# Six token groups of 384 in place of nine of 256 in the last MoE block of a fused attention and MoE kernel

## The chip, the cores and the metric

The kernel runs on one core of one Trainium2 chip. The metric is the device time of one execution in microseconds (us), given as a median over runs; smaller is better.

## What is computed

Banded and pooled attention over `q`, `k`, `v` gives a matrix `x` of 2304 tokens by 512. A first MoE block (512 to 1024 to 512, with a soft-LU and a layer norm between its two products) is applied to it, and then the block that the change touches:

```
def _moe2_ref(x, w_in, w_out):      # x: 2304 x 512, w_in: 512 x 2048, w_out: 2048 x 512
    h = x @ w_in
    g = h * np.cos(h)
    return (g @ w_out).astype(np.float32)
```

## The kernel before

All products of the two MoE blocks are made in three matmuls (`mm3`): each operand is split into a high and a low fp32r part (`split`: ScalarE copies the high part, VectorE subtracts it from the source), and high by high, high by low and low by high are added up in PSUM.

The last block goes through the tokens in groups of `GT = 256`, nine of them, and in each group through the 16 tiles (`KF2`) of 128 hidden columns. One such pair (group, tile) is called a step here; there are 144. `h2(g, m)` makes one tile of `h` with `KD = 4` times `mm3`, 12 matmuls whose moving operand is 256 tokens wide. Then seven instructions in a chain turn it into `g`: ScalarE L825 (scaled copy to integer), VectorE L826, ScalarE L828 (Sin) and L829 (Square), VectorE L830, and the split, ScalarE L368 and VectorE L369. The split result lands in a ring of `RING = 4` slots in `Gh` and `Gl`. `o2(g, m)` multiplies it with the second weight: for each 128 tokens one `mm3` with a moving operand 512 wide, so 6 matmuls, which accumulate over the 16 tiles in the PSUM tiles `oa` and `ob`. After the last tile ScalarE copies the results (L845) to `X`, and the SP queue sends them out. The program issues `h2` two steps ahead of `o2` (`LAG = 2`).

The split input of a group lies in `xh`/`xl`; a second buffer lies in the unused half of `Gh`/`Gl` (`xs`), so the split of the next group is issued in the middle of the current one.

While the first group of this block runs, `w2o_step` still loads and converts the second weight into `R1`, which held the weights of the first block, and before that the first weight goes into `w2i_h`/`w2i_l`. The last work of the first MoE block on PE is `x2`, which reads `Gh`/`Gl`.

The order on each engine is not the program's. `arrange` builds the graph of dependences, prices each instruction with a formula, works out due times, tries list schedules forwards and backwards for `ROUNDS = 20` rounds, and fixes the best order on every engine. A change of shapes therefore moves instructions elsewhere too. Lines 376 to 378 are the three matmuls of `mm3`, which all products share, so the trace is read by tile names (`h2a`, `h2b`, `oa`, `ob`, and `x` for `x2`).

Of the kernel before, what the change touches and what calls it, by code (L numbers as in the profile page):

```python
# [8 lines left out]
F32 = mybir.dt.float32  # L9
F32R = mybir.dt.float32r  # L10
# [10 lines left out]
QB = 64  # L21
# [9 lines left out]
LAG, RING = 2, 4  # L33
# [279 lines left out]
def kernel(  # L313
# [16 lines left out]
    NT, DM = out.shape  # L330
    DFF = w1i.shape[1]
    DFF2 = w2i.shape[1]
    KD = DM // 128
    KF = DFF // 128
    KF2 = DFF2 // 128
    NG = NT // GT
# [6 lines left out]
    wts = Turns(ctx.enter_context(tc.tile_pool(name="wts", bufs=1)), 1)  # L343
    moe = Turns(ctx.enter_context(tc.tile_pool(name="moe", bufs=2)), 2)
# [13 lines left out]
    w2o_s = R1.rearrange("p (k a f) -> p k a f", k=KF2, a=2)  # L358

    X = wts.tile([128, NT // QB, KD, QB], F32, name="X")  # L360
    Gh = wts.tile([128, KF, GT], F32R, name="Gh")
    Gl = wts.tile([128, KF, GT], F32R, name="Gl")
    xs = [[moe.tile([128, 2, KD, 128], F32R, name=f"x{j}", bufs=1) for j in "hl"]]

    def split(hi, lo, src, gain=None):

        if gain is None:
            nc.scalar.activation(out=hi, in_=src, func=AF.Copy)  # L368
            nc.vector.tensor_tensor(out=lo, in0=src, in1=hi.bitcast(F32), op=ALU.subtract)  # L369
        else:  # L370
            nc.scalar.activation(out=hi, in_=src, func=AF.Copy, scale=gain)
            nc.vector.scalar_tensor_tensor(out=lo, in0=src, scalar=gain, in1=hi.bitcast(F32),
                                           op0=ALU.mult, op1=ALU.subtract)

    def mm3(ps, lh, ll, rh, rl, start, stop):
        nc.tensor.matmul(ps, lh, rh, start=start, stop=False)  # L376
        nc.tensor.matmul(ps, lh, rl, start=False, stop=False)  # L377
        nc.tensor.matmul(ps, ll, rh, start=False, stop=stop)  # L378
# [8 lines left out]
    def bank(name):  # L387
        tag, bufs = BANKS[name]
        if tag in late:

            late[tag] += 1
            if late[tag] % 4 >= 2:
                tag = {"h1": "s", "m": "t"}[tag]
        return psum.tile([128, 512], F32, tag=tag, name=name, bufs=bufs)
# [204 lines left out]
    H = {}  # L599
    TB = 128 // QB  # L600

    def xsplit(g, t, d):

        x0 = (2 * g + t) * TB
        src = X[:, x0:x0 + TB].rearrange("p b k q -> p k b q")
        hi, lo = [x[:, t].rearrange("p k (b q) -> p k b q", b=TB) for x in (d["xh"], d["xl"])]
        split(hi, lo, src)

    def h1_half(g, t, half):
        d = H[g]  # L610
        ps = d[t, half] = bank("h1")
        f = slice(half * 512, (half + 1) * 512)
        for kk in range(KD):
            mm3(ps, d["xh"][:, t, kk, :], d["xl"][:, t, kk, :], w1i_h[:, kk, f], w1i_l[:, kk, f],
                kk == 0, kk == KD - 1)
        if half == 0:
            d[t, "m"] = small.tile([128, 4], F32, tag="m", name="m")
        nc.vector.reduce_max(out=d[t, "m"][:, half:half + 1], in_=ps, axis=AX.X)
# [29 lines left out]
    def ln_t(g, t):  # L648
        e = H[g][t, "e"]
        for i in range(2):  # L650
            ps = bank("lnT")
            for j in range(4):
                nc.tensor.transpose(ps[:, j * 128:(j + 1) * 128],
                                    e[:, (4 * i + j) * 128:(4 * i + j + 1) * 128], ident)
            s = slice(t * 128, (t + 1) * 128)
            split(Gh[:, 4 * i:4 * i + 4, s], Gl[:, 4 * i:4 * i + 4, s],
                  ps.rearrange("p (j q) -> p j q", j=4))

    def x2(g, c2):
# [34 lines left out]
    def globs(b, cc, *blocks):  # L694
        return [Glob(b, c, *blocks) for c in (2 * cc, 2 * cc + 1)] if b < B else []

    items, order, ends = [], [], {}
    for b in range(B):
        for t in range(NT3):
            new = [Loc(b, t, c) for c in range(NP)]  # L700
            ends[new[-1]] = b * S + (t + 1) * QT
            if b + t == 0:

                for cc in range(NPP):
                    a, g = new[2 * cc:2 * cc + 2], globs(0, cc, 0, 1)
# [12 lines left out]
    n_all, n_w1o = len(side), KF * DM // W1C  # L718
    msteps = []
    for g in range(NG + 1):  # L720
        H[g] = dict(xh=xs[0][0], xl=xs[0][1])
        for t in range(2):
            need = g * GT + (t + 1) * 128
            if g < NG:
                msteps.append((need, n_all, lambda g=g, t=t: xsplit(g, t, H[g])))
                msteps.append((need, n_w1o, lambda g=g, t=t: h1_half(g, t, 0)))
                msteps.append((need, n_w1o, lambda g=g, t=t: h1_half(g, t, 1)))
            if g > 0:
                msteps.append((0, n_all, lambda g=g, t=t: ln_t(g - 1, t)))
# [20 lines left out]
    n = len(items)  # L750
# [28 lines left out]
    w2i_h = w2.tile([128, KD, DFF2], F32R, name="w2i_h")  # L779
    w2i_l = w2.tile([128, KD, DFF2], F32R, name="w2i_l")  # L780
# [16 lines left out]
    def w2o_step(j):  # L797
        for f in range(0, DM, W2C):
            f = slice(f, f + W2C)
            split(w2o_s[:, j, 0, f], w2o_s[:, j, 1, f], wload(w2o[j * 128:(j + 1) * 128, f], raw2))  # L800

    late.clear()
    O = {}
    H.clear()
    xs.append([t[:, RING:RING + KD, :].rearrange("p k q -> p (k q)").rearrange("p (t k q) -> p t k q", t=2, k=KD)
               for t in (Gh, Gl)])

    def x2split(g):
        d = H[g] = {}
        d["xh"], d["xl"] = xs[g % 2]  # L810
        for t in range(2):
            xsplit(g, t, d)

    def h2(g, m):
        d = H[g]
        ps = bank(("h2a", "h2b")[m % 2])[:, :GT]
        s = slice(m * 128, (m + 1) * 128)
        for kk in range(KD):
            mm3(ps.rearrange("p (t q) -> p t q", t=2), w2i_h[:, kk, s], w2i_l[:, kk, s], d["xh"][:, :, kk, :], d["xl"][:, :, kk, :],
                kk == 0, kk == KD - 1)  # L820
        if m % 2 == 0:
            d["t"] = moe.tile([128, 4, GT], F32, tag="e", name="t")
        a, c = d["t"][:, 2 * (m % 2), :], d["t"][:, 2 * (m % 2) + 1, :]

        nc.scalar.activation(out=a.bitcast(I32), in_=ps, func=AF.Copy, scale=1.0 / TWO_PI)  # L825
        nc.vector.scalar_tensor_tensor(out=c, in0=a.bitcast(I32), scalar=-TWO_PI, in1=ps,  # L826
                                       op0=ALU.mult, op1=ALU.add)
        nc.scalar.activation(out=a, in_=c, func=AF.Sin, scale=0.5)  # L828
        nc.scalar.activation(out=c, in_=a, func=AF.Square, scale=2.0 ** 0.5)  # L829
        nc.vector.scalar_tensor_tensor(out=a, in0=c, scalar=1.0, in1=ps, op0=ALU.subtract, op1=ALU.mult,  # L830
                                       reverse0=True)
        split(Gh[:, m % RING, :], Gl[:, m % RING, :], a)

    def o2(g, m):
        if m == 0:
            O[g] = [bank("oa"), bank("ob")]
        for t in range(2):
            s = slice(t * 128, (t + 1) * 128)
            mm3(O[g][t], Gh[:, m % RING, s], Gl[:, m % RING, s], w2o_s[:, m, 0, :], w2o_s[:, m, 1, :],
                m == 0, m == KF2 - 1)  # L840
        if m == KF2 - 1:
            for t in range(2):
                x0 = (2 * g + t) * TB
                xo = X[:, x0:x0 + TB].rearrange("p b k q -> p (b k q)")
                nc.scalar.copy(out=xo, in_=O[g][t])  # L845
                r0 = g * GT + t * 128
                nc.sync.dma_start(out=out[r0:r0 + 128, :], in_=xo)

    seq = [(g, m) for g in range(NG) for m in range(KF2)]
    x2split(0)  # L850
    for i in range(len(seq) + LAG):
        if i < len(seq):
            g, m = seq[i]
            if m == KF2 // 2 and g + 1 < NG:
                x2split(g + 1)
            h2(g, m)
            if g == 0:
                w2o_step(m)
        if i >= LAG:
            o2(*seq[i - LAG])  # L860
# [59 lines left out]
```

## Time and profile before

| what | value |
|---|---|
| median of 3 runs | 787.16 us (786.53 to 787.47) |
| span of the profiled execution | 786.5 us, its first to its last instruction |
| PE busy | 768.7 us, 98% of the span |
| DVE, ACT busy | 521.3 us (66%), 470.9 us (60%) |
| granted TensorE clock | full over nearly the whole span (mean 1.000) |

The profiled execution has no time beside its span; the runs lie between that span and 0.9 us above it, the median 0.6 us above. PE stands for TensorE's matmuls, PEld for its weight loads, DVE for VectorE, ACT for ScalarE, SP for the queue that issues the transfers. The attention and the first block take about 376 us, the last block the rest.

### The profile page before, as it was taken

The numbers are of one execution on the slowest core, as the hardware profiler recorded it, in microseconds if no ns is written. First come the engines' busy times: TensorE is split into PE (matmuls) and PEld (weight loads), VectorE is DVE, ScalarE is ACT, GpSimd is POOL, SyncE is SP. The second block draws the span as 40 slices with busy tenths as digits, with TensorE's granted clock in tenths as the row PEclk, the third lists the DMA queues.
The fourth block names the chain that finished last, engine by engine and source line by source line (L and its number), as shares of the span: only waits on it lengthen the run. The fifth ranks groups of instructions, "written<-read, shape, count | busy, mean of one in ns | idle before, by whom it ended". The sixth has DMA issues, their size and how long they took to land.

```text
span 786.5 us, 14898 instructions
## 1 busy us (share of the span) xinstructions
PE 768.7 (98%) x5636; PEld 676.4 (86%) x5636; DVE 521.3 (66%) x1461; ACT 470.9 (60%) x1366; POOL 20.5 (3%) x38
## 2 busy tenths in 40 slices
PE   6999999999999999999999999999999999999998
PEld 4667798888889899889899999999999999999997
DVE  4999999968365698998996454544544454444443
ACT  2567677647565445565776565665656566565654
POOL 2000001000000000000000000000000000000000
PEclk9999999999999999999999999999999999999999
DMA  9988936433122033333441000000000000000000
GB/s 242 280 228 234 217 94 195 119 85 81 33 62 55 16 126 115 110 106 109 134 138 38 1 28 1 1 28 1 28 1 28 1 1 28 1 28 1 28 1 27
DMA packets 50679, 59.89 MB, mean 76 GB/s; under 512 B 23312, under 2 KB 35888, under 8 KB 50608
## 3 DMA queue, kind: packets, MB, share of 16 engines
q1 hardware_dynamic: 50608, 58.95, 26.0%
q8 instruction: 44, 0.72, 0.4%
q14 instruction: 27, 0.22, 0.1%
HBM read 54.22 MB, written 4.72 MB: 75 GB/s over the span
## 4 chain that ended last, share of the span: by engine, by line
PE 82%; DVE 12%; ACT 2%; issue 2%; POOL 1%; DMA 1%; POOLq 0%; SPq 0%; DVEq 0%; ACTq 0%
PE h2b L378 4%; PE oa L376 4%; PE h2b L377 4%; PE h2a L377 4%; PE h2a L376 4%; PE ob L378 4%; PE h2b L376 4%; PE oa L377 4%; PE ob L377 4%; PE h2a L378 4%; PE ob L376 4%; PE oa L378 4%; PE ls L566 4%; PE h L376 3%; PE h L378 3%; PE h L377 3%
## 5 line engine op out<-in xcount | busy, mean ns | idle before, releaser
L369 DVE TENSOR_TENSOR Gl<-t,Gh 128x256 fp32r<-128x256 f32 x144 | 61.0, 424 | 57.7 <-ACT Gh L368 57.7
L368 ACT ACTIVATE Gh<-t 128x256 fp32r<-128x256 f32 x144 | 60.0, 417 | 59.5 <-DVE t L830 59.3
L828 ACT ACTIVATE t<-t 128x256 f32<-128x256 f32 x144 | 60.1, 418 | 57.9 <-DVE t L826 57.8
L376 PE MATMUL x<-Gh,R 128*128 128x256 f32 x288 | 82.2, 288 | 1.6 <-ACT Gh L368 1.5
L377 PE MATMUL x<-Gl,R 128*128 128x256 f32 x288 | 82.4, 287 | 1.1 <-DVE Gl L369 0.8
L378 PE MATMUL x<-Gh,R 128*128 128x256 f32 x288 | 82.2, 286 | 0.0
L830 DVE SCALAR_TENSOR_TENSOR t<-t,h2b 128x256 f32<-128x256 f32 x72 | 30.2, 420 | 59.0 <-ACT t L829 59.0
L830 DVE SCALAR_TENSOR_TENSOR t<-t,h2a 128x256 f32<-128x256 f32 x72 | 30.3, 420 | 56.4 <-ACT t L829 56.4
L829 ACT ACTIVATE t<-t 128x256 f32<-128x256 f32 x144 | 60.2, 418 | 4.2
L376 PE MATMUL h<-R,xh 128*128 128x512 f32 x144 | 59.3, 412 | 0.9 <-DVE e L633 0.8
L376 PE MATMUL oa<-R,Gh 128*128 128x512 f32 x144 | 57.1, 397 | 1.0 <-ACT Gh L368 1.0
L377 PE MATMUL h<-R,xh 128*128 128x512 f32 x144 | 57.9, 402 | 0.0
L378 PE MATMUL h<-R,xl 128*128 128x512 f32 x144 | 57.6, 400 | 0.0
L376 PEld LDWEIGHTS x<-Gh,R 128*128 128x128 f32 x288 | 54.7, 191 | 3.1 <-ACT Gh L368 2.1
L377 PEld LDWEIGHTS x<-Gl,R 128*128 128x128 f32 x288 | 54.9, 191 | 2.6 <-DVE Gl L369 1.8
L378 PE MATMUL ob<-R,Gl 128*128 128x512 f32 x144 | 57.1, 397 | 0.0
L377 PE MATMUL oa<-R,Gh 128*128 128x512 f32 x144 | 56.9, 395 | 0.0
L377 PE MATMUL ob<-R,Gh 128*128 128x512 f32 x144 | 56.6, 393 | 0.0
L376 PE MATMUL ob<-R,Gh 128*128 128x512 f32 x144 | 56.3, 391 | 0.0
L378 PE MATMUL oa<-R,Gl 128*128 128x512 f32 x144 | 55.9, 388 | 0.0
L378 PEld LDWEIGHTS x<-Gh,R 128*128 128x128 f32 x288 | 54.9, 191 | 0.4
L452 ACT ACTIVATE le<-ls,sm 128x70 f32<-128x70 f32 x144 | 44.1, 320 | 14.1 <-PE lt L574 11.6
(123 smaller groups left out, 2188.9 us busy)
## 6 DMA issues: line engine op xcount, KB each, us to landing
wr<-in_w2i_dram SPq DMA_DIRECT2D x32, 256.0 KB
wr<-in_w2o_dram SPq DMA_DIRECT2D x32, 256.0 KB
lv<-in_vl_dram SPq DMA_DIRECT2D x48, 105.0 KB
kt<-in_k_dram SPq DMA_DIRECT2D x8, 594.0 KB
kw<-in_k_dram SPq DMA_DIRECT2D x24, 198.0 KB
qt<-in_q_dram SPq DMA_DIRECT2D x8, 576.0 KB
diag<-in_q_dram SPq DMA_DIRECT2D x48, 96.0 KB
gv<-in_vg_dram SPq DMA_DIRECT2D x16, 288.0 KB
```

The lines of the kernel that those rows point to most:

```text
L368: nc.scalar.activation(out=hi, in_=src, func=AF.Copy)
L369: nc.vector.tensor_tensor(out=lo, in0=src, in1=hi.bitcast(F32), op=ALU.subtract)
L376: nc.tensor.matmul(ps, lh, rh, start=start, stop=False)
L377: nc.tensor.matmul(ps, lh, rl, start=False, stop=False)
L378: nc.tensor.matmul(ps, ll, rh, start=False, stop=stop)
L452: nc.scalar.activation(out=e[:, j, :], in_=src[:, j, :], func=AF.Exp, bias=neg[:, j:j + 1], scale=scale, accum_out=ssum[:, j:j + 1])
L566: nc.tensor.matmul(ps[:, a * WIN:(a + 1) * WIN], self.d["q"][:, self.h, a].rearrange("p j s -> p (j s)"), self.d["k"][:, self.h, a * QB:a ...
L828: nc.scalar.activation(out=a, in_=c, func=AF.Sin, scale=0.5)
L829: nc.scalar.activation(out=c, in_=a, func=AF.Square, scale=2.0 ** 0.5)
L830: nc.vector.scalar_tensor_tensor(out=a, in0=c, scalar=1.0, in1=ps, op0=ALU.subtract, op1=ALU.mult, reverse0=True)
```

## The change

The last block takes `T2 = 384` tokens at a time, six groups, 96 steps. `h2` has 12 matmuls 384 wide, `o2` has three 128-token tiles with 9 matmuls 512 wide, and its three results take turns in the four PSUM buffers of `oa` and `ob`. One tile `P` takes the place of `Gh`, `Gl`, `xh` and `xl`; for the last block it is cut anew into two rings (`gh`, `gl`) and one buffer for the split input (`x2s`), in reverse order of its four parts (`KD - 1 - kk`). There is no second buffer: the split of a group is issued at its first step, part by part (four splits 384 wide in place of two 512 wide). A step has its own tile `t`, where two steps shared one.

```diff
+T2 = 384
-    Gh = wts.tile([128, KF, GT], F32R, name="Gh")
-    Gl = wts.tile([128, KF, GT], F32R, name="Gl")
-    xs = [[moe.tile([128, 2, KD, 128], F32R, name=f"x{j}", bufs=1) for j in "hl"]]
+    P = wts.tile([128, 2 * (KF + KD) * GT], F32R, name="P")
...
+    Gh, Gl = part(0, KF, GT), part(KF * GT, KF, GT)
+    xh1, xl1 = [part((2 * KF + i * KD) * GT, 2, KD, 128) for i in range(2)]
+    gh, gl = part(0, RING, T2), part(RING * T2, RING, T2)
+    x2s = part(2 * RING * T2, KD, 2, T2)
...
+    G2 = [(t, min(T2, NT - t)) for t in range(0, NT, T2)]
     def x2split(g):
-        d = H[g] = {}
-        d["xh"], d["xl"] = xs[g % 2]
-        for t in range(2):
-            xsplit(g, t, d)
+        t0, n = G2[g]
+        b0, nb = t0 // QB, n // QB
+        d = H[g] = []
+        for kk in range(KD):
+            src = X[:, b0:b0 + nb, kk, :]
+            d.append([x2s[:, KD - 1 - kk, i, :n] for i in range(2)])
+            split(*[x.rearrange("p (b q) -> p b q", q=QB) for x in d[kk]], src)
     def h2(g, m):
...
-            mm3(ps.rearrange("p (t q) -> p t q", t=2), w2i_h[:, kk, s], w2i_l[:, kk, s], d["xh"][:, :, kk, :], d["xl"][:, :, kk, :],
-                kk == 0, kk == KD - 1)
-        if m % 2 == 0:
-            d["t"] = moe.tile([128, 4, GT], F32, tag="e", name="t")
+            hi, lo = H[g][kk]
+            mm3(ps, w2i_h[:, kk, s], w2i_l[:, kk, s], hi, lo, kk == 0, kk == KD - 1)
+        t = moe.tile([128, 2, T2], F32, tag="e", name="t")
...
     def o2(g, m):
-            O[g] = [bank("oa"), bank("ob")]
-        for t in range(2):
+            O[g] = [bank(("oa", "ob")[(t0 // 128 + t) // 2 % 2]) for t in range(n // 128)]
+        for t in range(n // 128):
...
-    seq = [(g, m) for g in range(NG) for m in range(KF2)]
-    x2split(0)
+    seq = [(g, m) for g in range(len(G2)) for m in range(KF2)]
     for i in range(len(seq) + LAG):
         if i < len(seq):
             g, m = seq[i]
-            if m == KF2 // 2 and g + 1 < NG:
-                x2split(g + 1)
+            if m == 0:
+                x2split(g)
```

Lines after the new function are 12 to 14 higher in the changed kernel: the matmuls are L388 to L390, the split L380 and L381, the chain L838 to L843.

The first place is ScalarE at the border between the two blocks, around the end of the first block's last `x2`. Before (`R1` is the second weight, `t_4954` step 0's work tile, `h2a_4941` step 0's PSUM tile):

```order
L825 ACTIVATE t_4954<-h2a_4941 128x256 [waits PE_49]
L368 ACTIVATE R1_70<-wu_5035 128x256 [waits DVE_49]
L368 ACTIVATE R1_70<-wu_5043 128x256 [waits DVE_49]
L828 ACT_TABLE_LOAD [waits DVE_49]
L828 ACTIVATE t_4954<-t_4954 128x256 [waits Activation_49]
L368 ACTIVATE R1_70<-wu_5079 128x256 [waits DVE_49]
L829 ACTIVATE t_4954<-t_4954 128x256 [waits Activation_49]
L368 ACTIVATE R1_70<-wu_5087 128x256 [waits DVE_49]
L666 COPY X_71<-x2_4837 128x2x4x64 [waits PE_49]
```

The same place now (`P_72<-X_71` are the parts of the split input that lie where `Gl` lay, `t_4955` and `h2a_4942` belong to step 0, `h2b_4979` to step 1):

```order
L380 ACTIVATE P_72<-X_71 128x384 [waits PE_49]
L380 ACTIVATE R1_70<-wu_5186 128x256 [waits DVE_49]
L380 ACTIVATE P_72<-X_71 128x384 [waits PE_49]
L678 COPY X_71<-x2_4834 128x2x4x64 [waits PE_49]
L678 COPY X_71<-x2_4884 128x2x4x64 [waits PE_49]
L380 ACTIVATE R1_70<-wu_5224 128x256 [waits DVE_49]
L838 ACTIVATE t_4955<-h2a_4942 128x384 [waits PE_49]
L380 ACTIVATE R1_70<-wu_5232 128x256 [waits DVE_49]
L838 ACTIVATE t_4992<-h2b_4979 128x384 [waits PE_49]
L841 ACT_TABLE_LOAD
L841 ACTIVATE t_4955<-t_4955 128x384 [waits DVE_49]
```

Step 0's chain with its table load stood ahead of the copies of the last `x2` tiles and now stands behind them, since two parts of the first split wait for that `x2`.

The second place is PE where the first group ends and the second begins. Before (`ob_5052` is the first group's result, `h2a_5672` the second group's step 0, whose input lies in the second buffer):

```order
L376 MATMUL ob_5052<-R1_70,Gh_72 128x512
L377 MATMUL ob_5052<-R1_70,Gh_72 128x512
L378 MATMUL ob_5052<-R1_70,Gl_73 128x512
L376 MATMUL h2a_5672<-Gh_72,w2i_h_3738 128x256 [waits PE_49]
L377 MATMUL h2a_5672<-Gl_73,w2i_h_3738 128x256
L378 MATMUL h2a_5672<-Gh_72,w2i_l_3739 128x256
L376 MATMUL h2a_5672<-Gh_72,w2i_h_3738 128x256
```

The same place now (`P_72` is the split input and the ring alike):

```order
L390 MATMUL ob_5055<-R1_70,P_72 128x512
L388 MATMUL h2a_5671<-P_72,w2i_h_3735 128x384 [waits Activation_49]
L389 MATMUL h2a_5671<-P_72,w2i_h_3735 128x384 [waits DVE_49]
L390 MATMUL h2a_5671<-P_72,w2i_l_3736 128x384
L388 MATMUL h2a_5671<-P_72,w2i_h_3735 128x384 [waits Activation_49]
L389 MATMUL h2a_5671<-P_72,w2i_h_3735 128x384 [waits DVE_49]
L390 MATMUL h2a_5671<-P_72,w2i_l_3736 128x384
```

Each of the four parts of the new group's input now has its own pair of waits, and the nine `o2` matmuls of one step stand between the last `h2` of the old group and them.

The third place is ScalarE at the same border. Before (`t_5628` is the work tile of the first group's steps 14 and 15, `h2a_5615` and `h2b_5642` their PSUM tiles):

```order
L825 ACTIVATE t_5628<-h2a_5615 128x256 [waits PE_49]
L828 ACTIVATE t_5628<-t_5628 128x256 [waits DVE_49]
L829 ACTIVATE t_5628<-t_5628 128x256 [waits Activation_49]
L368 ACTIVATE Gh_72<-t_5628 128x256 [waits DVE_49]
L825 ACTIVATE t_5628<-h2b_5642 128x256 [waits PE_49]
```

The same place now (`t_5584` is step 14's work tile, `t_5630` and `h2b_5617` belong to step 15, and `P_72<-X_71` are the four parts of the second group's split):

```order
L838 ACTIVATE t_5584<-h2a_5571 128x384 [waits PE_49]
L841 ACTIVATE t_5584<-t_5584 128x384 [waits DVE_49]
L842 ACTIVATE t_5584<-t_5584 128x384 [waits Activation_49]
L380 ACTIVATE P_72<-X_71 128x384 [waits PE_49]
L380 ACTIVATE P_72<-t_5584 128x384 [waits DVE_49]
L380 ACTIVATE P_72<-X_71 128x384 [waits PE_49] x3
L838 ACTIVATE t_5630<-h2b_5617 128x384
```

The four copies of the second group's split now stand between the chains of steps 14 and 15, the first of them ahead of the end of step 14's chain; before, the second group's split stood at the border of the two blocks.

## Rows read from the trace of the kernel before

**Rows 1.** The page: engines' busy time, and the span in 40 slices.

```profile
PE 768.7 (98%) x5636; PEld 676.4 (86%) x5636; DVE 521.3 (66%) x1461; ACT 470.9 (60%) x1366; POOL 20.5 (3%) x38
...
PE   6999999999999999999999999999999999999998
...
PEclk9999999999999999999999999999999999999999
```

**Rows 2.** Stretches of the span: length, busy us (instructions) by engine, clock, DMA.

```profile
300.00:384.00 84.00, 79.82 (x566) 73.70 (x565) 78.39 (x227) 46.97 (x109) 5.34 (x6) 1.00 0.37 117
384.00:425.00 41.00, 41.00 (x264) 37.32 (x263) 38.02 (x116) 29.90 (x80) 0.00 (x0) 1.00 0.31 103
425.00:775.00 350.00, 350.00 (x2227) 317.83 (x2226) 163.03 (x385) 212.89 (x522) 0.00 (x0) 1.00 0.03 12
```

**Rows 3.** PE in order of time, last block: start, duration, first matmuls of steps.

```profile
389.45 0.28 PE L376 MATMUL h2a<-xh,w2i_h 128*128 128x256 f32 x1
...
400.77 0.28 PE L376 MATMUL h2a<-xh,w2i_h 128*128 128x256 f32 x1
...
402.21 0.40 PE L376 MATMUL oa<-R,Gh 128*128 128x512 f32 x1
...
403.59 0.29 PE L376 MATMUL h2b<-xh,w2i_h 128*128 128x256 f32 x1
...
774.33 0.28 PE L376 MATMUL h2a<-xh,w2i_h 128*128 128x256 f32 x1
```

**Rows 4.** PE in order of time: bf16 matmuls 350 wide that keep PE busy.

```profile
29.75 0.31 PE L689 MATMUL idle<-mask,identb 128*128 128x350 bf16 x1
31.02 0.91 PE L689 MATMUL idle<-mask,identb 128*128 128x350 bf16 x5
```

**Rows 5.** PE in order of time at the border of the two blocks.

```profile
361.97 0.66 PE L653 MATMUL lnT<-ident,e 128*128 128x128 f32 x4 [0.64 <-ACT X L666]
...
363.75 0.39 PE L376 MATMUL x<-Gh,R 128*128 128x256 f32 x1 [0.17 <-DVE Gl L369]
...
375.84 0.28 PE L378 MATMUL x<-Gh,R 128*128 128x256 f32 x1
375.96 0.28 PE L376 MATMUL h2b<-xh,w2i_h 128*128 128x256 f32 x1
...
382.66 0.50 PE L376 MATMUL oa<-R,Gh 128*128 128x512 f32 x1 [0.99 <-ACT Gh L368]
```

**Rows 6.** Groups on ACT and DVE, 430 to 786 us: count, busy us, mean ns.

```profile
L368 ACT ACTIVATE Gh<-t 128x256 fp32r<-128x256 f32 x125 | 52.2, 418 | 57.0 <-DVE t L830 57.0
L829 ACT ACTIVATE t<-t 128x256 f32<-128x256 f32 x124 | 51.9, 418 | 3.7
...
L825 ACT ACTIVATE t<-h2b 128x256 int32<-128x256 f32 x62 | 23.7, 383 | 10.2 <-PE h2b L378 10.1
...
L845 ACT COPY X<-oa 128x512 f32<-128x512 f32 x8 | 4.7, 587 | 3.4 <-PE oa L378 3.4
...
L368 ACT ACTIVATE xh<-X 128x512 fp32r<-128x512 f32 x6 | 3.4, 623 | 0.0
...
L369 DVE TENSOR_TENSOR Gl<-t,Gh 128x256 fp32r<-128x256 f32 x125 | 53.1, 425 | 56.6 <-ACT Gh L368 56.6
...
L830 DVE SCALAR_TENSOR_TENSOR t<-t,h2b 128x256 f32<-128x256 f32 x63 | 26.5, 421 | 57.5 <-ACT t L829 57.5
...
L369 DVE TENSOR_TENSOR Gl<-X,Gh 128x512 fp32r<-128x512 f32 x6 | 3.9, 690 | 0.3
```

**Rows 7.** Groups on ACT, 300 to 384 us: the table load, weight splits.

```profile
L368 ACT ACTIVATE R<-wu 128x256 fp32r<-128x256 f32 x14 | 5.8, 416 | 10.8 <-DVE wu L414 10.7
...
L828 ACT ACT_TABLE_LOAD x1 | 1.3, 1283 | 0.3 <-DVE t L826 0.3
```

**Rows 8.** The end, in order of time: PE, then ACT, then DVE.

```profile
777.53 0.28 PE L378 MATMUL h2b<-xh,w2i_l 128*128 128x256 f32 x1
...
782.44 0.39 PE L378 MATMUL ob<-R,Gl 128*128 128x512 f32 x1
...
777.85 0.39 ACT L825 ACTIVATE t<-h2b 128x256 int32<-128x256 f32 x1
...
782.87 0.58 ACT L845 COPY X<-ob 128x512 f32<-128x512 f32 x1 [0.55 <-PE ob L378]
...
780.53 0.42 DVE L369 TENSOR_TENSOR Gl<-t,Gh 128x256 fp32r<-128x256 f32 x1 [0.48 <-ACT Gh L368]
```

More of the change, by code (lines that the diff above doesn't have):

```diff
@@ L360, with part @@
     X = wts.tile([128, NT // QB, KD, QB], F32, name="X")
-    Gh = wts.tile([128, KF, GT], F32R, name="Gh")
-    Gl = wts.tile([128, KF, GT], F32R, name="Gl")
-    xs = [[moe.tile([128, 2, KD, 128], F32R, name=f"x{j}", bufs=1) for j in "hl"]]
+    P = wts.tile([128, 2 * (KF + KD) * GT], F32R, name="P")
+    def part(at, *shape):
+        n = 1
+        for x in shape:
+            n *= x
+        names = "abcd"[:len(shape)]
+        return P[:, at:at + n].rearrange(f"p ({' '.join(names)}) -> p {' '.join(names)}", **dict(zip(names[1:], shape[1:])))
+    Gh, Gl = part(0, KF, GT), part(KF * GT, KF, GT)
+    xh1, xl1 = [part((2 * KF + i * KD) * GT, 2, KD, 128) for i in range(2)]
+    gh, gl = part(0, RING, T2), part(RING * T2, RING, T2)
+    x2s = part(2 * RING * T2, KD, 2, T2)
     def split(hi, lo, src, gain=None):
@@ L720 @@
     for g in range(NG + 1):
-        H[g] = dict(xh=xs[0][0], xl=xs[0][1])
+        H[g] = dict(xh=xh1, xl=xl1)
         for t in range(2):
@@ L804 @@
     H.clear()
-    xs.append([t[:, RING:RING + KD, :].rearrange("p k q -> p (k q)").rearrange("p (t k q) -> p t k q", t=2, k=KD)
-               for t in (Gh, Gl)])
+    G2 = [(t, min(T2, NT - t)) for t in range(0, NT, T2)]
     def x2split(g):
-        d = H[g] = {}
-        d["xh"], d["xl"] = xs[g % 2]
-        for t in range(2):
-            xsplit(g, t, d)
+        t0, n = G2[g]
[5 more added lines that the diff above has]
+            split(*[x.rearrange("p (b q) -> p b q", q=QB) for x in d[kk]], src)
     def h2(g, m):
-        d = H[g]
-        ps = bank(("h2a", "h2b")[m % 2])[:, :GT]
+        n = G2[g][1]
+        ps = bank(("h2a", "h2b")[m % 2])[:, :n]
         s = slice(m * 128, (m + 1) * 128)
         for kk in range(KD):
-            mm3(ps.rearrange("p (t q) -> p t q", t=2), w2i_h[:, kk, s], w2i_l[:, kk, s], d["xh"][:, :, kk, :], d["xl"][:, :, kk, :],
-                kk == 0, kk == KD - 1)
-        if m % 2 == 0:
-            d["t"] = moe.tile([128, 4, GT], F32, tag="e", name="t")
-        a, c = d["t"][:, 2 * (m % 2), :], d["t"][:, 2 * (m % 2) + 1, :]
+            hi, lo = H[g][kk]
+            mm3(ps, w2i_h[:, kk, s], w2i_l[:, kk, s], hi, lo, kk == 0, kk == KD - 1)
+        t = moe.tile([128, 2, T2], F32, tag="e", name="t")
+        a, c = t[:, 0, :n], t[:, 1, :n]
         nc.scalar.activation(out=a.bitcast(I32), in_=ps, func=AF.Copy, scale=1.0 / TWO_PI)
@@ L831, in h2 @@
                                        reverse0=True)
-        split(Gh[:, m % RING, :], Gl[:, m % RING, :], a)
+        split(gh[:, m % RING, :n], gl[:, m % RING, :n], a)
     def o2(g, m):
+        t0, n = G2[g]
         if m == 0:
-            O[g] = [bank("oa"), bank("ob")]
-        for t in range(2):
+            O[g] = [bank(("oa", "ob")[(t0 // 128 + t) // 2 % 2]) for t in range(n // 128)]
+        for t in range(n // 128):
             s = slice(t * 128, (t + 1) * 128)
-            mm3(O[g][t], Gh[:, m % RING, s], Gl[:, m % RING, s], w2o_s[:, m, 0, :], w2o_s[:, m, 1, :],
+            mm3(O[g][t], gh[:, m % RING, s], gl[:, m % RING, s], w2o_s[:, m, 0, :], w2o_s[:, m, 1, :],
                 m == 0, m == KF2 - 1)
         if m == KF2 - 1:
-            for t in range(2):
-                x0 = (2 * g + t) * TB
-                xo = X[:, x0:x0 + TB].rearrange("p b k q -> p (b k q)")
+            for t in range(n // 128):
+                r0 = t0 + t * 128
+                xo = X[:, r0 // QB:r0 // QB + TB].rearrange("p b k q -> p (b k q)")
                 nc.scalar.copy(out=xo, in_=O[g][t])
-                r0 = g * GT + t * 128
                 nc.sync.dma_start(out=out[r0:r0 + 128, :], in_=xo)
-    seq = [(g, m) for g in range(NG) for m in range(KF2)]
-    x2split(0)
+    seq = [(g, m) for g in range(len(G2)) for m in range(KF2)]
     for i in range(len(seq) + LAG):
```

## The prediction, on record before the changed kernel ran

> **What bounds the kernel now.** First the page: PE is busy 98% of the span at the full granted clock, DVE 66%, ACT 60% [rows 1]. That is a mean, so the stretches come next [rows 2]. From 384 us on, through the block that changes, PE is busy 41.00 of 41.00 us and 350.00 of 350.00, while DVE has 163 us of work in the 350 and ACT 213. PE waits for nobody there, and the length of the block is the number of its matmuls times the slot of each. From 300 to 384 us, around the border of the two blocks, it is another matter: DVE is busy 78.4 of 84 us, PE only 79.8, so 4.2 us of PE time are lost. The order in time names the last such waits: 0.64, 0.17 and 0.99 us [rows 5]. So two things count: what a matmul 384 wide costs, and whether the new order of the splits makes PE wait at the border of the blocks, at the five borders between groups, or at the end.
>
> **The price of a slot.** A busy matmul overlaps the next, so I take distances between starts, not durations. One step's 12 matmuls 256 wide go from 400.77 to 402.21, 1.44 us, and its 6 matmuls 512 wide from 402.21 to 403.59, 1.38 us [rows 3]. From 389.45 to 774.33 there are 136 such steps, 2.830 us each [rows 3]; spreading the 0.01 us that the mean has more, a slot is 120.4 ns at 256 and 230.8 ns at 512. A straight line through both has 110.4 / 256 = 0.431 ns a column and a fixed 2 x 120.4 - 230.8 = 10.0 ns a matmul. At 384 it gives 120.4 + 55.2 = 175.6 ns.
>
> No row has an fp32r matmul 384 wide. Bounds: from 256 up with 128 columns at one a tick of 2.4 GHz (53.3 ns) it is 173.7; from 512 down by the same it is 177.5. I take the line's 175.6, since nothing favours either end. That a width between is not charged as 512 is seen in bf16: four slots 350 wide take 0.91 - 0.31 = 0.60 us, 150 ns each [rows 4].
>
> **The sum for PE.** `o2` is unchanged in work: 864 matmuls 512 wide before and after. `h2` goes from 144 x 12 = 1728 matmuls at 120.4 ns (208.0 us) to 96 x 12 = 1152 at 175.6 ns (202.3 us). That is 5.8 us less (576 fixed parts of 10.0 ns), 3.5 at the upper bound, 8.0 at the lower.
>
> [...]
>
> **The chains beside it.** ACT and DVE do the same columns in fewer instructions. By the line between the 256 and 512 rows an ACT copy 384 wide takes (418 + 623) / 2 = 520 ns and a DVE subtraction (425 + 690) / 2 = 558 ns; L825's 383 becomes about 485, L830's 421 about 555 [rows 6]. A step gives ACT about 2.05 us and DVE 1.67 us in a step of PE of 12 x 175.6 + 9 x 230.8 = 4.18 us, so PE stays the bound. One step's chain before went from the last `h2` start at 777.53 to the end of L369 at 780.95, 3.4 us [rows 8]; its seven operations become 3.7 us in place of 2.9, so 4.2 us. Between `h2` and `o2` of a step PE has two `o2` steps and two `h2` steps, 8.4 us, which covers it.
>
> **The border of the blocks.** Two of the four parts of the first split lie where `Gl` lay and wait for the last `x2`; so step 0 can't be finished early, as it was. PE: the last `x2` starts at 375.84 and `h2` goes on at 375.96 [rows 5]. 10 of the 48 matmuls of steps 0 to 3 stand ahead of that, 38 behind: 38 x 175.6 = 6.67 us, so PE would reach the first `o2` at 382.6. ACT: step 0's tile is done 13 matmuls behind the `x2`, at 375.96 + 13 x 0.1756 = 378.2; ACT follows the last start by 0.32 us (777.53 to 777.85 [rows 8]), so at 378.4. Then come L838 (0.49), a weight split (0.42), L838 of step 1 (0.49), the table load for Sin, 1.28 us [rows 7], Sin and Square of steps 0 and 1 (4 x 0.52), and the copy of step 0's result (0.52): 378.4 + 5.3 = 383.7. The table load was hidden by `x2` before; now PE waits for it, 1.2 us in place of the 0.99 at 382.66 [rows 5]. The waits on the parts of the split I price at 0.1: the ACT copies of both parts and the weight split between them (1.5 us from 375.3) end at about 376.7, when PE comes to them, five matmuls behind the last `x2`. Together +0.3 us. Below, this could be nothing; above, if DVE and ACT are late by a whole weight split on each side, +1.5.
>
> **The borders between groups.** The split has one buffer, so its first part waits until step 15 has read that part. PE then has the other three parts of step 15 (9 x 0.176 = 1.6 us) and nine `o2` matmuls (2.08 us) ahead. Counted from the end of step 15 on PE, ACT can start the first part at -1.3 us, then the copy of step 14, then three parts: five times 0.52 us, done at 1.4; DVE follows with the last subtraction at 2.1. PE asks for the first part at 2.1, when it is long there, and for the last low part at 2.1 + 10 x 0.176 = 3.8. So 1.7 us are to spare and I cost it at nothing. What is late next is step 15's chain, 1.1 us, inside its 8.4. The new group's `oa` and `ob` wait for copies of 0.58 us [rows 6]; three of them have six `o2` and twelve `h2` matmuls (3.5 us) as cover.
>
> **The end.** The last `h2` is followed by 20 `o2` matmuls (4.6 us) before the first that needs step 15's high part, which is there after about 3.7 us. From the last matmul's start (782.44 [rows 8]) to the end of the span stay 4.1 us: one copy, one transfer. Nothing changes.
>
> **The first block.** The planner's best order differs from about 215 us on. The same work stands ahead of the last layer-norm split on DVE (the sum of its durations differs by 0.1 us), but single steps move by up to 2 us. I cost it at 0, with 1 us either way out of the 4.2 us that PE loses there [rows 2].
>
> **Sum.** Span 786.5 - 5.8 + 0.3 = 781.0 us. The median lies 0.6 us above that span, so 787.2 - 5.5 = 781.7 us.
>
> **Rivals.** (1) Only a small part of a slot is fixed. The bf16 slot of 150 ns has 4 ns over its 350 columns at 2.4 GHz [rows 4]. If no more than that is fixed in fp32r and the rest goes with the columns, 384 costs 4 + 1.5 x 116.4 = 178.6 ns, the gain on PE is 208.0 - 205.7 = 2.3, and the time 787.2 - 2.3 + 0.3 = 785.2 us. Against it: at 512 such a slot would be 4 + 2 x 116.4 = 236.8, where 230.8 stands. [...] (2) The borders between groups show: if the split were only begun when step 15 is over, four copies and a subtraction (0.3 + 4 x 0.52 + 0.56 = 2.9 us) outlast the 2.1 us of cover by 0.9 us, five times, 4.4 us: 786.1 us. For it: one buffer and in-order ACT. Against it: each part has its own wait in the order, and ACT is busy 61% [rows 2]. (3) Slower: a width that is no multiple of 256 pays for a second piece, 256 and 128 each with the fixed 10 ns, 185.6 ns a slot. That is 1152 x 10.0 = 11.5 us more: 793.2 us. It decides from 180.4 ns on (5.5 / 1152 = 4.8 ns over the line). Against it: 512 costs less than twice 256, so pieces pay nothing there; no row speaks for it but that none has this width.
>
> **Chances.** Forecast 0.76, rival 1 0.11, rival 2 0.07, rival 3 0.06. The forecast's own cases run from 778.8 (lower slot, -8.0, and nearly 1 us of luck in the first block) to 785.2 (upper slot, -3.5, with 1.5 of loss at the border); about half of rival 1 lies at that end, and the other half, 2 and 3 above it. So 778.8 to 785.2 is the range. Within 0.2% (1.6 us, about what a measurement of this kernel can tell from no change) are half of rival 1 and rival 2: faster 0.80, same 0.13, slower 0.07.
>
> **What would show it.** Slots of 175 to 176 ns between `h2` starts; a step of 4.18 us; no PE wait from 390 us on; one wait of about 1.2 us of the first `oa` for ACT behind the table load. A slot of 178 or more proves rival 1, waits of PE on the split's ACT or DVE at five places rival 2, over 180 rival 3. Waits of more than 5 us in the first block would make me wrong in a way that I have not priced.

## The result and the profile after

The changed kernel takes 780.47 us (median of 4 runs, 779.07 to 781.03), the kernel before 787.08 in the runs beside it (786.53 to 787.47): a ratio of 0.9912, 95% interval 0.9896 to 0.9929. Five more runs of the changed kernel gave 779.57 us and 0.9917 (0.9904 to 0.9929). So it is faster by 6.5 to 6.9 us. The prediction was 781.7 us, 5.5 us faster.

The page of the changed kernel, in answer to [rows 1]:

```profile
span 777.3 us, 13499 instructions
PE 760.9 (98%) x5060; PEld 669.4 (86%) x5060; DVE 500.9 (64%) x1323; ACT 437.8 (56%) x1180; POOL 20.0 (3%) x38
...
PEclk9999999999999999999999999999999999999999
```

PE is still busy 98% of the span at the full granted clock. It has 576 matmuls fewer, and DVE and ACT are less busy. The stretches, with the columns of [rows 2]:

```profile
300.00:384.00 84.00, 81.83 (x556) 75.65 (x556) 80.26 (x231) 48.12 (x110) 4.74 (x6) 1.00 0.38 117
384.00:425.00 41.00, 41.00 (x207) 37.03 (x206) 33.57 (x91) 25.37 (x56) 0.00 (x0) 1.00 0.27 84
425.00:775.00 350.00, 348.57 (x1741) 315.02 (x1739) 146.54 (x268) 186.19 (x368) 0.00 (x0) 1.00 0.04 14
```

From 384 us on PE never waits; 348.57 of 350 is only the earlier end, since its last matmul ends at 773.58. New is the first row: from 300 to 384 us PE loses 2.2 us, not 4.2. PE in order of time in the last block, in answer to [rows 3] and [rows 8] (start, duration):

```profile
391.37 0.34 PE L388 MATMUL h2a<-P,w2i_h 128*128 128x384 f32 x1
...
399.77 0.34 PE L388 MATMUL h2a<-P,w2i_h 128*128 128x384 f32 x1
...
401.89 0.39 PE L388 MATMUL oa<-R,P 128*128 128x512 f32 x1
...
403.97 0.34 PE L388 MATMUL h2b<-P,w2i_h 128*128 128x384 f32 x1
...
760.97 0.34 PE L388 MATMUL h2a<-P,w2i_h 128*128 128x384 f32 x1
...
773.19 0.39 PE L390 MATMUL oa<-R,P 128*128 128x512 f32 x1
```

From 391.37 to 760.97 there are 88 steps, 4.200 us each. Over all distances between neighbouring starts from 430 to 765 us (those over 0.6 us left out), the mean slot is as follows; the kernels of the experiments stand below.

| kernel | 256 columns | 384 | 512 |
|---|---|---|---|
| before | 120.39 ns | | 230.89 |
| changed | | 176.25 | 231.66 |
| groups of 256, one buffer (two kernels) | 120.38 | | 230.90 |
| groups of 512 | | | 231.4 |

12 x 176.25 + 9 x 231.66 = 4.200 us, so the slots account for the whole step. Against before that is 144 x 2.830 - 96 x 4.200 = 4.3 us: 5.0 less in `h2`, 0.7 more in `o2`. It shows in the trace as a whole: from the last `x2` matmul to the last matmul there were 406.6 us (375.84 to 782.44 in [rows 5] and [rows 8]), and now there are 402.3.

The rest came earlier. All waits of PE that the profile names from 300 to 375 us in before (waited for: us in total, times, longest):

```profile
PE x L376 <- ACT Gh L368: 1.5, 1, 1.5
PE lnT L653 <- ACT X L666: 0.6, 1, 0.6
PE x L377 <- DVE Gl L369: 0.6, 2, 0.4
PE x L377 <- DVE m L625: 0.3, 1, 0.3
PE x L376 <- DVE Gl L369: 0.2, 1, 0.2
```

And in the changed kernel:

```profile
PE lnT L665 <- ACT X L678: 0.6, 1, 0.6
PE x L388 <- ACT P L380: 0.4, 1, 0.4
PE x L389 <- DVE P L381: 0.2, 1, 0.2
```

3.2 us became 1.2. These are matmuls of the first block, whose computation is not changed, waiting for their split operands. To compare the two executions a landmark is needed: the matmuls are counted from 0 in order of their starts, without the bf16 ones of [rows 4]. Number 2000 starts at 243.22 us before and at 241.22 after, and the last `x2` comes 132.6 us behind it before and 129.7 after, 2.9 us less. Number 2000 is not the same instruction in both kernels, since the order differs there. Number 250 is, the second of these two matmuls, before and after:

```profile
45.53 0.38 PE L522 MATMUL gt<-ident,ge 128*72 128x128 f32 x2
43.64 0.38 PE L534 MATMUL gt<-ident,ge 128*72 128x128 f32 x2
```

From it to the last `x2` it is 330.2 and 327.2 us, 3.0 less. That both numbers come 2 us earlier after is not the change's, as the experiments show.

### The profile page after: what moved, and what is told of

Read it like the earlier page. It is cut to its first block, busy times and chain, and to the rows that moved or that the text cites. A ratio compares the mean times of both kernels' runs of the same rounds, so it can differ in the third digit from the quotient of the medians.

```text
span 777.3 us, 13499 instructions
## 1 busy us (share of the span) xinstructions
PE 760.9 (98%) x5060; PEld 669.4 (86%) x5060; DVE 500.9 (64%) x1323; ACT 437.8 (56%) x1180; POOL 20.0 (3%) x38
## 4 chain that ended last, share of the span: by engine, by line
PE 83%; DVE 11%; ACT 2%; issue 1%; POOL 1%; DMA 0%; POOLq 0%; DVEq 0%; SPq 0%; ACTq 0%
PE oa L390 5%; PE oa L389 5%; PE oa L388 5%; PE h2a L390 4%; PE h2b L390 4%; PE h2a L388 4%; PE h2a L389 4%; PE h2b L389 4%; PE h2b L388 4%; PE ob L390 4%; PE ob L389 4%; PE ob L388 4%; PE ls L578 4%; PE h L388 3%; PE h L390 3%; PE h L389 3%
## 5 line engine op out<-in xcount | busy, mean ns | idle before, releaser
L381 DVE TENSOR_TENSOR P<-t,P 128x384 fp32r<-128x384 f32 x96 | 53.5, 557 | 47.6 <-ACT P L380 47.5
L389 PE MATMUL x<-P,R 128*128 128x256 f32 x288 | 82.3, 287 | 0.3 <-DVE P L381 0.2
L390 PE MATMUL x<-P,R 128*128 128x256 f32 x288 | 82.0, 286 | 0.0
L388 PE MATMUL x<-P,R 128*128 128x256 f32 x288 | 81.6, 286 | 0.4 <-ACT P L380 0.4
L841 ACT ACTIVATE t<-t 128x384 f32<-128x384 f32 x96 | 50.4, 525 | 54.2 <-DVE t L839 54.1
L380 ACT ACTIVATE P<-t 128x384 fp32r<-128x384 f32 x96 | 50.3, 523 | 50.4 <-DVE t L843 49.8
L390 PE MATMUL h2a<-P,w2i_l 128*128 128x384 f32 x192 | 65.1, 339 | 0.0
L390 PE MATMUL h2b<-P,w2i_l 128*128 128x384 f32 x192 | 65.1, 339 | 0.0
L389 PE MATMUL h2a<-P,w2i_h 128*128 128x384 f32 x192 | 64.9, 338 | 0.0
L389 PE MATMUL h2b<-P,w2i_h 128*128 128x384 f32 x192 | 64.9, 338 | 0.0
L388 PE MATMUL h2a<-P,w2i_h 128*128 128x384 f32 x192 | 64.8, 337 | 0.0
L388 PE MATMUL h2b<-P,w2i_h 128*128 128x384 f32 x192 | 64.7, 337 | 0.0
L390 PE MATMUL oa<-R,P 128*128 128x512 f32 x160 | 63.5, 397 | 0.0
L389 PE MATMUL oa<-R,P 128*128 128x512 f32 x160 | 63.1, 395 | 0.0
L388 PE MATMUL oa<-R,P 128*128 128x512 f32 x160 | 62.1, 389 | 0.8 <-ACT P L380 0.8
L388 PE MATMUL h<-R,P 128*128 128x512 f32 x144 | 59.3, 411 | 0.9 <-DVE e L645 0.8
L843 DVE SCALAR_TENSOR_TENSOR t<-t,h2b 128x384 f32<-128x384 f32 x48 | 26.6, 553 | 50.6 <-ACT t L842 50.6
L843 DVE SCALAR_TENSOR_TENSOR t<-t,h2a 128x384 f32<-128x384 f32 x48 | 26.6, 553 | 49.5 <-ACT t L842 49.5
L389 PE MATMUL h<-R,P 128*128 128x512 f32 x144 | 58.0, 403 | 0.0
L390 PE MATMUL h<-R,P 128*128 128x512 f32 x144 | 57.6, 400 | 0.0
L388 PEld LDWEIGHTS x<-P,R 128*128 128x128 f32 x288 | 54.7, 191 | 1.6 <-ACT P L380 1.1
L389 PEld LDWEIGHTS x<-P,R 128*128 128x128 f32 x288 | 54.8, 191 | 1.4 <-DVE P L381 1.0
```

## The experiments

The expectations call the last `x2` matmul, which ends the first block, "the last transpose": a wrong name. In all kernels but one (the changed kernel again, which is not edited) the order ahead of the last block is set by hand: the planned starts of the 3992 steps that both programs share and of the 192 steps that split the last block's second weights are overwritten by those planned for the one or the other kernel, and each engine takes its steps in the order of planned starts.

```diff
+    begun.update(zip(steps[:SHARED] + later, given))
+    for s in steps:
+        begun[s] = max([begun[s]] + [begun[a] for a in s.preds])
+    kept = {e: sorted(order, key=lambda s: (begun[s], s.at)) for e, order in kept.items()}
```

**The changed kernel again.** 

> The changed kernel once more, with nothing edited, beside the others on the same chip. Ratio to before 0.990 to 0.993 (780.5 us where before is at 787.1). Its trace shows what differs from one execution to another: if the first 45 us, where it and the kernel before have the same instructions, start 2 us later or earlier again, then as much of a difference between single traces is not the change's. The stretch from the last transpose to the last matmul should be 402.3 us within 0.3, and the mean slot of a matmul of 384 columns 176.2 ns within 0.3, if these are the kernel's and not the execution's.

Measured: 779.57 us, ratio 0.9917 (0.9904 to 0.9929). The last `x2` comes 129.75 us after matmul 2000, then 402.26 us follow to the last matmul; the 384 slot is 176.24 ns. So these are the kernel's own. Matmul 250 of the profiled executions started at 45.6 us before, at 43.7 here, at 43.8 in the first profile of the changed kernel, and at 45.8 in the run with the early Sin below, whose instructions up to there are the same. So an execution has 2 us of start-up more or less. The profiled execution of before was one with more. The times of before, 785.8 to 788.8 us, scatter as widely; that the start-up is the reason there too is likely and not shown, since those runs have no trace.

**The changed kernel with the old order of the first block.** The planned starts put in are those of before.

> The changed kernel with one thing put back: each engine takes the steps ahead of the last block in the order of the kernel before. Theory A (the order ahead of the last block gives 2 to 2.7 us): the stretch from the last transpose to the last matmul stays at 402.3 us, the last transpose starts 2 to 2.7 us later than in the changed kernel, and the time is 782.5 to 783.2 us (ratio to before 0.994 to 0.995). Rival B (the order does nothing): 780.5 us, within 0.7 (ratio 0.9916).

Measured: 782.14 us, ratio 0.9945 (0.9932 to 0.9957), 2.6 us over the changed kernel beside it. PE's waits from 300 to 375 us:

```profile
PE lnT L833 <- ACT X L846: 1.0, 1, 1.0
PE x L556 <- ACT P L548: 0.8, 1, 0.8
PE x L557 <- DVE m L805: 0.3, 1, 0.3
PE x L557 <- DVE P L549: 0.2, 1, 0.2
```

They are 2.3 us again instead of 1.2, and the last `x2` comes 132.0 us after matmul 2000, 2.3 us later than with the new order (2.4 from matmul 250). The named waits are 1.1 us of that, and one `h2` matmul more ahead of the last `x2` (11 instead of 10) is 0.2; the rest lies in starts that come late without a named wait. From there to the end it takes 402.6 us, against 402.3 in the changed kernel. Theory A holds: the order ahead of the last block is worth 2.3 us in the trace up to the last `x2` and 2.6 in the medians.

**The kernel before with the new order.** The same edit on before, with the planned starts of the changed kernel.

> The kernel before with one thing of the changed kernel: the order in which each engine takes the steps of the first MoE block and of all that stands ahead of the last block. The last block keeps nine groups of 256. From the start of the last transpose of the last block's input to the start of the last matmul the trace of before has 406.6 us and that of the changed kernel 402.3 us. Theory A: the changed kernel's gain is 4.3 us in the last block's slots and a further 2 to 2.7 us from this order, because TensorE waits less between 300 and 371 us. Then the last transpose starts 2 to 2.7 us earlier than in before, the stretch behind it stays at 406.6 us, and the time falls from 787.1 to 784.4 to 785.1 us (ratio 0.9966 to 0.9975). Rival B: the order does nothing, and the earlier start of the last block came from the start-up of the profiled execution, which differed by 2 us in the first 45 us where both programs are the same. Then the time stays at 787.1 us, within 0.7.

Measured: 786.08 us, ratio 0.9996 (0.9986 to 1.0005), which by the time is rival B. But the trace shows both halves. The last `x2` comes 130.6 us after matmul 2000, 2.0 us earlier than in before, and PE's waits to 375 us are 1.6 us instead of 3.2. Behind it, to the last matmul, it is 408.1 us instead of 406.6. PE in order of time there:

```profile
377.85 0.28 PE L546 MATMUL h2a<-xh,w2i_l 128*128 128x256 f32 x1
379.74 0.50 PE L544 MATMUL oa<-R,Gh 128*128 128x512 f32 x1 [1.61 <-ACT Gh L536]
```

The wait of 0.99 us [rows 5] is 1.61 here, and smaller ones follow. So theory A's first half holds and its sum fails: with nine groups of 256 most of the gain is lost again at the border of the blocks. These planned starts also move the weight splits there on ACT and DVE; that these cause it was not tried by itself.

**Groups of 256 in the changed kernel.** One line, with the new order held:

```diff
-T2 = 384
+T2 = 256
```

> The changed kernel with groups of 256 instead of 384 in the last block, so nine groups again, but with the one shared buffer and with a split of each part of the input on its own, and the order ahead of the last block held as in the changed kernel. Theory A (the width alone makes the last block shorter, by the fixed part of a matmul's slot): 1728 matmuls of 256 columns at 120.4 ns take 208.0 us where 1152 of 384 at 176.25 take 203.0, so the stretch from the last transpose to the last matmul is 406.5 to 407.5 us instead of 402.3, and the time 784.5 to 785.5 us (ratio to before 0.996 to 0.998). Rival B (the one buffer and the splits by part make it shorter): the stretch stays near 402.3 us and the time at 780.5. Beside it: the outputs' matmuls of 512 columns took 230.9 ns in before and 231.7 in the changed kernel; if this comes from the width of what stands between them it is 230.9 here, if from the buffer 231.7.

Measured: 789.78 us, ratio 1.0036 (1.0021 to 1.0052), slower than both theories said. The slots are 120.38 and 230.90 ns, as theory A says and as in before; but the split input now lies over low parts that the first block reads to its end. The last block's first matmul came at 370.8 us instead of 356.4, and PE waited besides. So the place was mended:

```diff
-    x2s = part(2 * RING * T2, KD, 2, T2)
+    x2s = part(2 * (KF + KD) * GT - 2 * KD * T2, KD, 2, T2)
```

> The run with groups of 256 and one buffer once more, with its split input at the end of the buffer (where the first block's split tokens were) instead of over the first block's low parts, which are read up to the last x2 matmul; there the last block's first matmul had come at 370.8 us instead of 356.4, and the time was 789.8 us, worse than either theory said, though the slots were 120.4 and 230.9 ns. The order ahead of the last block is that of the changed kernel. Theory A (the width gives 4 to 4.5 us in the last block, the place of the buffer had cost the rest): the last block starts before the last x2 matmuls again, and the stretch from the last transpose to the last matmul is 406 to 407.5 us, the time 784.5 to 785.5 us (ratio to before 0.996 to 0.998). Rival B (the one buffer itself costs at 256, since a part's split must wait for the group before to have read it): TensorE waits at the eight borders of groups, 0.3 to 0.6 us each, and the time is 787 to 790 us.

Measured: 787.14 us, ratio 0.9999 (0.9990 to 1.0008), so no gain over before is left. The slots are again 120.38 and 230.91. Between the last `x2` and the last matmul are 408.4 us. PE's waits from 300 to 425 us:

```profile
PE lnT L833 <- ACT X L846: 1.8, 1, 1.8
PE oa L556 <- ACT P L548: 1.1, 1, 1.1
PE x L556 <- ACT P L548: 0.6, 2, 0.4
PE h2a L557 <- DVE P L549: 0.4, 1, 0.4
PE x L557 <- DVE P L549: 0.3, 1, 0.3
```

Theory A had the slots right, and 406 to 407.5 us too low; rival B had the time, but for the wrong place. The wait of `h2a` is at the first border of groups, where the starts from 415.3 to 418.0 us lie 1.7 us further apart in all than slots do. The seven later borders have none. The other loss is the 1.8 us of `lnT`, 0.6 in the changed kernel. From matmul 2000 to the last matmul this kernel takes 8.0 us more than the changed one (7.6 in the medians): 4.3 are slots, 1.7 this border, 0.3 the longer wait of the first `o2` (1.1 instead of 0.8), and the rest comes ahead of the last `x2`.

**The table load put earlier.** A Sin of one column ahead of the first group's work, so that the table is there when it is needed:

```diff
         a, c = t[:, 0, :n], t[:, 1, :n]
+        if g == m == 0:
+            nc.scalar.activation(out=c[:, 0:1], in_=nhalf, func=AF.Sin)
```

> The changed kernel with one more instruction: a Sin of one column on ScalarE ahead of the first group's work, so that the table load of 1.28 us, which stands in the chain ahead of the first output matmul of the last block, comes while TensorE still runs the first 24 matmuls. The order of all steps ahead of the last block is held as in the changed kernel. Theory A: that chain is what the first output matmul waited 0.84 us for, and the load is in it, so the wait goes to 0 to 0.1 us and the stretch from the last transpose to the last matmul falls from 402.3 to 401.4 to 401.6 us; the time is 779.7 us (ratio 0.9906). Rival B: another link binds as well (the transposes' copies before it, or the squares behind it), the wait stays over 0.5 us and the time at 780.5 us. In the times of the runs the two are hard to tell apart; the wait in the trace tells it.

In the changed kernel ACT does this between the last `x2` and the first `o2`:

```profile
371.09 0.51 ACT L380 ACTIVATE P<-X 128x384 fp32r<-128x384 f32 x1
371.50 1.05 ACT L678 COPY X<-x 128x512 f32<-128x512 f32 x2
...
374.41 0.49 ACT L838 ACTIVATE t<-h2b 128x384 int32<-128x384 f32 x1
374.92 1.28 ACT L841 ACT_TABLE_LOAD   x1
376.21 0.53 ACT L841 ACTIVATE t<-t 128x384 f32<-128x384 f32 x1
...
378.17 0.51 ACT L380 ACTIVATE P<-t 128x384 fp32r<-128x384 f32 x1
```

And this is PE there, in answer to [rows 5]:

```profile
370.79 0.41 PE L390 MATMUL x<-P,R 128*128 128x256 f32 x2
371.04 0.34 PE L388 MATMUL h2b<-P,w2i_h 128*128 128x384 f32 x1
...
377.55 0.34 PE L390 MATMUL h2b<-P,w2i_l 128*128 128x384 f32 x1
378.73 0.50 PE L388 MATMUL oa<-R,P 128*128 128x512 f32 x1 [0.84 <-ACT P L380]
```

With the early Sin PE has no wait from 372 us on, and the last `x2` to the last matmul takes 401.6 us instead of 402.3: theory A. The time is 780.27 us, ratio 0.9922 (0.9909 to 0.9936), no better, and from matmul 2000 to the last matmul the trace has 532.0 us as in the changed kernel, so as much was lost ahead of the last `x2`. The load stood in a bad place, as ACT's rows show:

```profile
359.79 1.09 ACT L548 ACTIVATE P<-lnT 128x512 fp32r<-128x512 f32 x2
360.89 1.28 ACT L1006 ACT_TABLE_LOAD   x1
362.19 0.20 ACT L1006 ACTIVATE t<-nhalf 128x1 f32<-128x1 f32 x1
362.30 0.58 ACT L548 ACTIVATE P<-lnT 128x512 fp32r<-128x512 f32 x1
```

There it stands ahead of the first block's last split. Held behind that split instead (the Sin's planned start set just after the last of them):

> As the run with the early Sin, where the load of the table stood at 360.9 us between two splits of the first block's last normalized tokens: there the first output matmul waited for nothing, and the stretch from the last transpose to the last matmul fell by 0.67 us to 401.6, but the last transpose came 0.7 us later. Here the same Sin is held behind the last of these splits, where ScalarE waits 1.4 to 1.9 us at a time. Theory A (the load only cost where it delayed those splits): the stretch is 401.6 us and the last transpose stands where it does in the changed kernel, so the time is 0.7 us under its own, 778.9 to 779.9 us (ratio 0.9908). Rival B (wherever the load stands, something on ScalarE's path comes as much later): as the changed kernel, ratio 0.9917. In the times the two can hardly be told apart; the trace tells them apart by the last transpose's start against the 2000th matmul's, 129.7 us in the changed kernel and 130.4 with the early Sin.

Measured: 779.82 us, ratio 0.9907 (0.9891 to 0.9923). PE waits for nothing from 372 us on, and the stretch is 401.5 us. The last `x2` comes 25.5 us after matmul 2750, as in the changed kernel; with the early Sin it was 25.95, so of the 0.7 us lost there 0.4 come from the place of the load. (From matmul 2000 to the last `x2` it is 130.1 us, not 129.7: 0.4 us were lost ahead of matmul 2750 at 346 us, where both kernels have the same instructions, so that is scatter.) Theory A by the trace, 0.7 us; in the times the intervals overlap.

**Groups of 512.** Four and one of 256. The first try had a ring of two for the split hidden values with the lag of two:

```diff
-T2 = 384
+T2 = 512
-LAG, RING = 2, 4
+LAG, RING = 2, 2
```

> The changed kernel with groups of 512 in the last block (four of them and one of 256) and a ring of two in place of four for its split hidden values, which is what fits. Theory A (the fixed part of a slot is all that the width buys): 768 matmuls of 512 columns at 231 ns and 192 of 256 at 120.4 take 200.5 us where 1152 of 384 at 176.25 take 203.0, so the stretch from the last transpose to the last matmul is 399.8 us instead of 402.3, and the time 778.0 us (ratio 0.9885). Rival B (a border of groups costs): with four output banks per group no spare bank is left, and with a ring of two a split waits for the output matmuls of two steps before; then TensorE waits 0.3 to 1 us at each of four borders, or at every step, and the stretch is 401 to 404 us, the time 779 to 782.

Here each output step reads the hidden values of two steps later, so its waits are those of another computation: 782.31 us, and 781.24 with the later Sin. Neither says anything on the width. With the output one step behind (`LAG, RING = 1, 2`):

> Groups of 512 (four and one of 256) with a ring of two for the split hidden values and the output matmuls one step behind the hidden ones instead of two. (In the two runs before with groups of 512 the lag was two with a ring of two, so that each output step read the hidden values of two steps later; their waits are of another computation.) Theory A (the fixed part of a slot is what the width buys, and one step of 5.5 us covers the chain on ScalarE and VectorE of some 5 us): 768 matmuls of 512 at 231 ns and 192 of 256 at 120.4 take 200.5 us where 1152 of 384 took 203.0; time 778.0 us (ratio 0.9885). Rival B (the chain of one step on ScalarE and VectorE is longer than the step, or the border of blocks and groups has nothing between): TensorE waits 0.2 us or more in each of 72 steps, or over 1 us at each border, and the time is at or over 780.5 us, up to 795.

Measured: 778.65 us, ratio 0.9897 (0.9883 to 0.9911). PE in order of time, one step:

```profile
499.92 0.40 PE L556 MATMUL oa<-R,P 128*128 128x512 f32 x1
...
502.68 0.40 PE L556 MATMUL h2a<-P,w2i_h 128*128 128x512 f32 x1
...
505.48 0.40 PE L556 MATMUL oa<-R,P 128*128 128x512 f32 x1
```

24 matmuls in 5.56 us, 231.7 ns each. From the last `x2` to the last matmul it is 400.7 us, 1.6 less than with 384, of the 2.5 that theory A promised. PE's waits from 372 us on:

```profile
PE oa L558 <- DVE P L549: 0.4, 2, 0.2
PE h2a L557 <- DVE P L549: 0.2, 1, 0.2
```

Where starts lie further apart than a slot (at 373, 384, 393, 394 and 400 us, with the next start each time) it is 2.1 us in all, and behind 401 us nothing waits. The changed kernel has 1.1 us of this kind, at 378.73. So theory A holds but for the first steps, and the 1.0 us between the two sums accounts for the 0.9 us that it lacks. In the times the intervals of 384 and 512 overlap; the trace tells the two apart.

> The same with the Sin of one column behind the first block's last splits. Theory A: the first output matmul of the last block follows one hidden step earlier than with a lag of two, so that the chain with the table load stands open there; the early load takes 1.0 to 1.3 us from the first wait, and the time is that much under groups of 512 without it (777.0 us if that is 778.0). Rival B: other links of the chain bind and it is under 0.3 us.

Measured: 778.13 us, ratio 0.9892 (0.9875 to 0.9908), the lowest median of all, and 400.4 us from the last `x2`: 0.3 us less, so rival B. The first `oa` waited hardly at all without the Sin, so there was little to take.

## Why the prediction was right, step by step

The time, 781.7 us predicted and 780.47 measured, was right by terms that were off in opposite directions: PE's gain in the last block was forecast 1.5 us too high, the first block's gain was left out, 2.3 us, and the border was charged 0.3 us that it did not cost. That these nearly cancel is luck; that the slots are the larger part of the gain was foreseen.

**The price of a slot** was nearly right: 175.6 ns predicted from the line, 176.25 measured, inside the bounds of 173.7 and 177.5. The 0.65 ns are 0.8 us over 1152 matmuls, so `h2` gave 5.0 us, 8.7 ns for each of the 576 matmuls saved instead of 10.0.

**"`o2` is unchanged in work"** was right, but its price was not: 231.66 ns a slot instead of 230.89, 0.7 us over 864 matmuls. With groups of 256 in the same buffer it is 230.90, so it comes with the groups of 384 and not with the buffer. Whether with the width of the matmuls between or with nine `o2` matmuls in a row in place of six, no run tells. The term of PE was mis-sized: 4.3 us instead of 5.8, still within its bounds of 3.5 and 8.0.

**The first block** was the step that failed: "I cost it at 0, with 1 us either way". The new order of steps whose work had not changed gave 2.3 us by the run that takes it back, and 2.6 in the medians. That lay in the 4.2 us that PE lost from 300 to 384 us, which I had read from the row and then only bounded by a guess. With it the sum closes: 4.3 + 2.3 is 6.6, where 6.5 to 6.9 was measured. The single trace of before has 2.9 in place of 2.3; the 0.6 us between them is not explained, beside a scatter of 0.4 that two traces of the same instructions showed.

**The border of the blocks** held in its mechanism: ACT let the first `o2` start 7.8 us behind the last `x2`, 378.73 less 370.92. The prediction had 383.7 less 375.84, 7.9 us, with the table load in it. The wait was 0.84 us instead of 1.2, since PE came a little later; the prediction's own figures, 383.7 less 382.6, give 1.1. Beside the 0.99 us of before that is a gain of 0.15 us and not the loss of 0.3 that the sum has. That the load is in the chain was shown by moving it ahead: the wait went.

**The groups' borders and the end** cost nothing, as said: the profile names no wait of PE after 378.73, and from the last matmul's start to the end of the span there are 4.1 us in both kernels. ACT and DVE at 384 columns came out as the line between the rows gave them (predicted 558, 520, 520 and 555 ns, in the order of these rows):

```profile
L381 DVE TENSOR_TENSOR P<-t,P 128x384 fp32r<-128x384 f32 x96 | 53.5, 557 | 47.6 <-ACT P L380 47.5
L841 ACT ACTIVATE t<-t 128x384 f32<-128x384 f32 x96 | 50.4, 525 | 54.2 <-DVE t L839 54.1
L380 ACT ACTIVATE P<-t 128x384 fp32r<-128x384 f32 x96 | 50.3, 523 | 50.4 <-DVE t L843 49.8
...
L843 DVE SCALAR_TENSOR_TENSOR t<-t,h2b 128x384 f32<-128x384 f32 x48 | 26.6, 553 | 50.6 <-ACT t L842 50.6
```

These rows of the changed kernel's page, over the whole span, answer [rows 6].

**From the span to the time** was off by 1.5 us. In the later runs of before the time lies 2.1 us above the span (787.57 and 785.5, for one), not 0.6; in the changed kernel it is 1.8 (779.07 and 777.3), within 0.1 in all its runs. So some 0.3 us of the gain lie outside the span, which no part of the prediction had. The 0.6 us that I took between the span of before and the median compared an execution of long start-up with a median of others. As the gain was taken off the median, this did no harm.

**Rivals.** 176.25 ns lies nearer to the line's 175.6 than to rival 1's 178.6, and far from rival 3's 185.6. By rival 1's price `h2` would have gained 2.3 us where the trace has 5.0. Rival 2, five waits at the groups' borders, has none. It was not far-fetched: with groups of 256 in one buffer the first border cost 1.7 us.

What stays open: why the planner's new order suits PE better, why a slot of 512 columns costs 0.8 ns more in the kernel with groups of 384, and what makes the start-up longer or shorter.

## What to carry to other kernels

Where a matmul-bound stage has a fixed part in each slot, wider moving operands buy that part and no more. Take it from distances between starts at two widths: the line gave 10.0 ns for each matmul saved, the trace 8.7. The line was off by 0.4% of a slot only, yet that was 0.8 of the 5.8 us forecast, since the gain is a small difference of large terms. Where a planner orders all engines together, a change in one block moves steps of another: price the PE waits of every stretch whose order changes, with all of them as the upper bound and not a guess, because that term may be half as large as the one the edit is about. A buffer shared with the stage before must lie where that stage is done first; the kernel with groups of 256 was 2.6 us faster with its input at the other end.

## What the runs showed of the hardware

The slot of an fp32r matmul has no constant fixed part: over the columns at 2.4 GHz it has 13.7 ns at 256, 16.3 at 384 and about 18 at 512. Executions that differ in nothing up to there reach matmul 250 at 43.6 to 47.1 us in the thirteen traces, and from there to matmul 2000 all of them take 197.5 or 197.6 us. From matmul 2000 to the last one the two traces of the changed kernel agree to 0.1 us, and the run with the later Sin lost 0.4 us at a place where its instructions are the same. So single profiles can't be compared by their spans alone.
